# Loads of the head in portions between SyncE's waits, and two visits of the retention part moved

## The chip, the cores and the metric

The kernel runs on one core of one Trainium2 chip. The metric is device time in microseconds (us) of one execution. The kernel before takes 954.64 us, the median of 3 runs (953.72 to 954.76).

## The reference, cut to what matters

```python
# attention part: B, H, S, D = 8, 8, 576, 64; no softmax
scores = scale * np.matmul(q, k.transpose(0, 1, 3, 2))
Dmat = np.where(rel >= 0, gamma[:, None, None] ** rel[None, :, :], 0.0)
attn_out = np.matmul(scores * Dmat[None], v)
x = attn_out.transpose(0, 2, 1, 3).reshape(B * S, H * D)     # 4608 tokens x 512
# dense part: w_in 512 x 2048, w_out 2048 x 512
h = x @ w_in
P = a[0] + a[1] * h + a[2] * h**2 + a[3] * h**3
Q = 1.0 + abs(b[0]) * abs(h) + abs(b[1]) * h**2
out = (P / (Q + 1e-06)) @ w_out
```

Decay by a power of gamma makes the attention part a retention: it can be worked off in pieces that hand on a state.

## The kernel before, in words

**Units.** The 4608 tokens are 36 units of 128 tokens. Unit k is loaded by two DMAs of 512 KB on SyncE's queue (`load_unit`, L115 and L117): `qk` holds q and k, transposed, and `kv` holds k and v. GpSimd scales q (`scale_q`), ScalarE scales v in 8 instructions, one a head (`scale_v`). TensorE then makes the unit's *scores* (from `qk`, in two halves of 64 tokens) and its *state* terms (from `kv`); in the function names both together are the visit of k. VectorE masks the scores and adds up the states (`decay`, `middle`, `add`), GpSimd fades the state by gamma (`fade`). TensorE makes the *outputs* of the unit from the masked scores, v, q and the state (`put`). ScalarE rounds them to a tile `xhi` (`keep_hi`), VectorE keeps the rest in `xlo` (`keep_lo`). Four units are one block of 512 tokens, the x of the dense part.

**Dense part.** It goes in 144 steps, one for each block and each of 16 slices of d_ff: 8 slices of block 0 (steps 0 to 7), all 16 of block 1 (8 to 23), the other 8 of block 0 (24 to 31), then the other blocks. A step makes h (`gemm1`, 12 matmuls of 128x512, from `xhi` and `xlo` with the weight's two parts), runs the rational function on ScalarE and VectorE (`ffn_p`, `ffn_p2`, `ffn_va`, `ffn_v`, `ffn_r`, `ffn_q`, `ffn_q3`), rounds the result to `g` (`ffn_hi`, `ffn_lo`), and three to four steps later multiplies it by w_out (`gemm2`, 12 matmuls). PSUM has two buffers `h`, which the visits of the dense part use as well (as `y`).

**Weights.** They come as float64 bits, 32 tiles `bits` of 512 KB (`load_weights`, L150), and each is converted once (`split_weight`): ScalarE takes the absolute value into `c`, VectorE makes a TENSOR_SCALAR and two SCALAR_TENSOR_TENSOR on it, ScalarE copies it to `w`, GpSimd subtracts to get the second part. `start` and `split0` to `split3` in the order lists are these moves; STARTS_BEFORE and STARTS say how many conversions begin in each step.

**Head.** Before the dense part, `before(n)` for n = 0 to 4 makes the scores of unit n and the outputs of unit n-1, by the list BEFORE, and for the last n by LAST_BEFORE: `visit_a` is the scores of unit n, `visit_b` the outputs of unit n-1. Short series of matmuls that nobody reads (`warm`) stand between them.

**Visits.** VISITS says in which step of the dense part the outputs of one unit and the scores of another are made. Steps 8 to 21 have none; there two halves of a PSUM tile of the retention part (tag `at`) hold the `u` of the steps (`free_at`). The list FIRST sets the order within a step up to step 23, DENSE from step 24.

**Queues.** TensorE, ScalarE, VectorE and GpSimd run in the order in which the code names their work. SyncE's DMAs are placed by the scheduler. DMAs on SyncE's queue have eight slots in turn: each waits until the DMA eight before it has landed. In `emit` the matmuls of a unit's outputs run on two row halves of the array at once; where one half writes a PSUM bank that the other writes too, it waits for the other through an empty instruction on SyncE (`nc.sync.nop()` and `follow`, L289). Such a *join* stands in SyncE's queue among the DMAs: it passes only when the DMAs placed ahead of it have been issued.

**Lines.** Compute instructions are all recorded by one helper (L72 in the profile of before), so groups go by tiles. Of loads, L115 and L117 are a unit's, L150 a weight's, L554 is the small `ab`.

Of the kernel before, what the change touches and what calls it, by code (L numbers as in the profile page):

```python
# [30 lines left out]
NP = 4  # L31

BEFORE = "split1 start scale_q scale_v visit_a decay visit_b add fade keep_hi keep_lo split2 split3 split0".split()
LAST_BEFORE = "visit_a visit_b keep_hi keep_lo start split1 decay add fade scale_q scale_v split2 split3 split0".split()
FIRST = (
    "split1 gemm1 visit ffn_p split2 ffn_p2 ffn_hi decay keep_hi ffn_lo gemm2 ffn_r scale_q split3 decay1 add fade keep_lo"
    " start scale_v split0 ffn_q ffn_q3 ffn_va ffn_v"
# [11 lines left out]
).split()  # L49
END = "ffn_r ffn_hi gemm2 ffn_lo ffn_q ffn_q3".split()  # L50

STARTS_BEFORE = [0, 1, 1, 2, 2]
STARTS = [1, 1, 2, 1, 2] + [1] * 19

VISITS = {0: (4, 5), 2: (5, 6), 4: (6, 7), 6: (7, None), 22: (None, 8)}
FIRST_DENSE = 22
VISITS |= {24 + 2 * i: (8 + i, 9 + i) for i in range(3)}
VISITS |= {30 + 4 * i: (11 + i, 12 + i if i < 24 else None) for i in range(25)}
WARM = [8, 3, 2]
# [16 lines left out]
def retention_ffn(ctx: ExitStack, tc: tile.TileContext, qkv, w_in, w_out, ab, masks, gq, gv, out):  # L76
# [10 lines left out]
    nc = tc.nc  # L87
# [21 lines left out]
    def load_unit(n):  # L109


        late = 2 <= n < 6
        pools = [(wts, f"w{w}_{10 + n}") if late else (raw, "qk" if w == 0 else "kv") for w in range(2)]
        qk = pools[0][0].tile([P, 2, NPAIR, P], F32, tag=pools[0][1], name=f"qk{n}")
        nc.sync.dma_start(qk, qkv[n, :, 0:1024].rearrange("p (a g i) -> p a g i", a=2, g=NPAIR))  # L115
        kv = pools[1][0].tile([P, 2, H, D], F32, tag=pools[1][1], name=f"kv{n}")
        nc.sync.dma_start(kv, qkv[n, :, 1024:2048].rearrange("p (a h d) -> p a h d", a=2, h=H))  # L117
        raws[n] = qk, kv
# [4 lines left out]
    ab_sb = const.tile([P, 6], F32, name="ab_sb")  # L123
# [6 lines left out]
    def warm(n, by=None):  # L130
        by = gq_sb[:, 0] if by is None else by
        for _ in range(n):
            pe.matmul(unread[:, 0:P], by, by, start=True, stop=True)
# [13 lines left out]
    def load_weight(k):  # L147

        bits[k] = wts.tile([P, DM], I64, tag=f"w{k[0]}_{k[1]}", name=f"bits{k[0]}_{k[1]}")
        nc.sync.dma_start(bits[k], (w_in, w_out)[k[0]][k[1]])  # L150
# [39 lines left out]
    def scale_q(n):  # L190

        q = raws[n][0][:, 0]
        pool.tensor_tensor(q, q, gq_sb, ALU.mult)
# [102 lines left out]
    def visit(a, k):  # L296


        places(a, k)
        if a is None:  # L300
            emit(of_scores(k, 0) + of_state(k, 0), of_scores(k, 1) + of_state(k, 1))
        elif k is None:
            put(a)
        else:
            one = of_inside(a, 0, 0) + of_before(a, 0) + of_scores(k, 0) + of_state(k, 0)
            two = of_inside(a, 1, 1) + of_before(a, 1) + of_scores(k, 1) + of_state(k, 1) + of_inside(a, 1, 0)
            one += [[]] * (len(two) - len(one) - 2) + of_inside(a, 0, 1)
            emit(one, two)
        if a is not None:
            done_with(a)  # L310

    def put(a):
        emit(*(of_inside(a, j, j) + of_before(a, j) + of_inside(a, j, 1 - j) for j in range(2)))

    def done_with(a):

        del raws[a]
        state.pop(a, None)
        if 6 <= a + 2 < NU:
            load_unit(a + 2)  # L320
# [185 lines left out]
    def load_weights(n):  # L506
        for k in [k for _, k in zip(range(n), loads)]:
            load_weight(k)
# [12 lines left out]
    def run(names, todo):  # L521
        todo |= {f"split{j}": (split_step, j) for j in range(4)}
        for name in names:
            if name in todo:
                todo[name][0](*todo[name][1:])

    def before(n):
        def start_scores():
            visit(None, n)
            if n + 1 < len(WARM):  # L530
                warm(WARM[n + 1])

        def start_outputs():
            put(n - 1)
            done_with(n - 1)
            if n < NP:
                warm(WARM_OUT)

        todo = {"visit_a": (start_scores,), "start": (split_start, STARTS_BEFORE[n])}
        todo |= {f.__name__: (f, n) for f in (decay, add, fade)}  # L540
        todo |= {f.__name__: (f, n + 1) for f in (scale_q, scale_v)}
        if n >= 1:
            todo |= {f.__name__: (f, n - 1) for f in (keep_hi, keep_lo)}
            todo["visit_b"] = (start_outputs,)
        run(BEFORE if n < NP else LAST_BEFORE, todo)

    nc.sync.dma_start(gq_sb, gq)
    load_unit(0)
    nc.sync.dma_start(gv_sb, gv)
    nc.sync.dma_start(mask_sb, masks)  # L550
    for n in range(1, 6):
        load_unit(n)
        load_weights(1 if n < 3 else 2)
    nc.sync.dma_start(ab_sb, ab)  # L554
    scale_q(0)
    scale_v(0)
    for n in range(NP + 1):
# [11 lines left out]
    for i in range(len(steps) + lag(len(steps))):  # L569
        this, prev, prev2 = (steps[j][:2] if 0 <= j < len(steps) else None for j in (i, i - 1, i - 2))  # L570
        todo = {"gemm2": (products, i), "start": (split_start, STARTS[i] if i < first else 0)}

        if i in VISITS:
            a, k = VISITS[i]
            todo["visit"] = visit, a, k
            if a is not None:
                todo |= {f.__name__: (f, a) for f in (keep_hi, keep_lo)}
            if k is not None:
                todo |= {f.__name__: (f, k) for f in (decay, decay1, add, fade)}
        if i + 1 in VISITS and VISITS[i + 1][1] is not None:  # L580
            todo |= {f.__name__: (f, VISITS[i + 1][1]) for f in (scale_q, scale_v)}
        if this:
# [53 lines left out]
```

## Time and profile before

| | |
|---|---|
| median of 3 runs | 954.64 us (953.72 to 954.76) |
| the profiled execution's own time | 955.94 us |
| its span, first to last instruction | 954.2 us |
| mean granted TensorE clock | 0.975 |
| DMA issues: units, weights, outputs | 72 and 32 of 512 KB, 16 and 4 of 512 and 256 KB |
| moved in the first three fortieths of the span | 334, 406, 334 GB/s |

A row of the timeline gives start, duration, engine, line, operation, output<-input, count, and in brackets how long the engine had been idle before it and what ended that. A row of the waits gives engine, tile, what it waited for, us in total, times and the longest. A row of the stages gives for each engine its busy time and number of instructions, then the granted clock, the share of the DMA engines and GB/s. PEld is TensorE's weight load, SPq SyncE's queue.

### The profile page before, as it was taken

The page shows a single profiled execution, that of the slowest core. Times are in us where ns is not written, and L with a number is a line of the kernel's source. Part 1 is how long each engine was busy: PE and PEld are TensorE (multiplying, and loading weights), DVE is VectorE, ACT ScalarE, POOL GpSimd, SP SyncE. Part 2 cuts the span into 40 slices and gives each one's busy share as a digit, 9 for nine tenths or more (in the row PEclk, how much of TensorE's full clock was granted, in tenths as well). Part 3 has the DMA queues.
Part 4 walks back from the last instruction along what each step waited for, and adds up shares of the span by engine and source line. Part 5 has one row for each costly group of instructions (what it writes and reads, how often), then busy time and mean ns, then how long its engine had stood idle before and what let it go on. Part 6 is the DMA issues. An engine that isn't in the chain of part 4 may idle for free.

```text
span 954.2 us, 19371 instructions
## 1 busy us (share of the span) xinstructions
PE 903.1 (95%) x7852; PEld 739.4 (77%) x7852; DVE 824.8 (86%) x1252; ACT 710.4 (74%) x1274; POOL 152.8 (16%) x128
## 2 busy tenths in 40 slices
PE   5769879979999999999999999999999999999998
PEld 4647658867888888888888888888888888888886
DVE  1699998988999898888888888888898889888895
ACT  3567688867777777877787778877877787867775
POOL 2354344434100000000000000000000000000000
PEclk9779999989999999999999999999999999999999
DMA  9981100001312111211121112111211121001001
GB/s 334 406 334 45 45 1 1 1 1 45 133 45 90 45 45 46 89 45 45 46 89 45 46 46 89 45 46 45 89 45 45 45 89 46 1 1 45 1 1 44
DMA packets 20568, 65.50 MB, mean 69 GB/s; under 512 B 2432, under 2 KB 2432, under 8 KB 20480
## 3 DMA queue, kind: packets, MB, share of 16 engines
q1 hardware_dynamic: 20480, 64.28, 18.9%
q8 instruction: 61, 1.00, 0.4%
q14 instruction: 27, 0.22, 0.1%
HBM read 54.83 MB, written 9.44 MB: 67 GB/s over the span
## 4 chain that ended last, share of the span: by engine, by line
PE 71%; DVE 4%; ACT 3%; issue 1%; DVEq 0%; ACTq 0%; SPq 0%
PE acc L72 34%; PE h L72 32%; PE ps L72 3%; PE y L72 2%; DVE p L72 1%; DVE v L72 1%; ACT kv L72 1%; ACT u L72 1%; DVE g L72 0%; DVE c L72 0%; DVE qk L72 0%; ACT v L72 0%; DVE xlo L72 0%; ACT p L72 0%; ACT g L72 0%
## 5 line engine op out<-in xcount | busy, mean ns | idle before, releaser
L72 PE MATMUL acc<-w,g 128*128 128x512 f32 x1632 | 401.9, 395 | 4.9 <-ACT o L72 3.6
L72 PE MATMUL h<-xhi,w 128*128 128x512 f32 x1152 | 384.0, 395 | 18.2 <-DVE p L72 17.5
L72 PEld LDWEIGHTS acc<-w,g 128*128 128x128 f32 x1632 | 307.1, 190 | 72.3 <-ACT o L72 4.1
L72 PEld LDWEIGHTS h<-xhi,w 128*128 128x128 f32 x1152 | 218.4, 190 | 71.9 <-DVE p L72 25.6
L72 PE MATMUL h<-xlo,w 128*128 128x512 f32 x576 | 226.1, 393 | 0.2 <-DVE xlo L72 0.2
L72 ACT ACTIVATE p<-h,ab_sb 128x512 f32<-128x512 f32 x144 | 111.4, 773 | 83.2 <-PE h L72 77.0
L72 ACT ACTIVATE u<-h 128x512 f32<-128x512 f32 x131 | 78.2, 597 | 89.0 <-DVE v L72 88.5
L72 DVE SCALAR_TENSOR_TENSOR p<-p,ab_sb,u 128x512 f32<-128x512 f32 x131 | 120.0, 916 | 25.8 <-ACT u L72 20.5
L72 PEld LDWEIGHTS h<-xlo,w 128*128 128x128 f32 x576 | 109.3, 190 | 22.5 <-DVE xlo L72 0.5
L72 DVE TENSOR_TENSOR v<-v,u 128x512 f32<-128x512 f32 x131 | 94.4, 721 | 28.3 <-ACT v L72 28.3
L72 DVE TENSOR_TENSOR p<-p,h 128x512 f32<-128x512 f32 x144 | 98.9, 686 | 19.6 <-ACT u L72 19.4
L72 DVE SCALAR_TENSOR_TENSOR p<-p,ab_sb,h 128x512 f32<-128x512 f32 x144 | 107.5, 747 | 4.7
L72 ACT ACTIVATE v<-u,absb 128x512 f32<-128x512 f32 x131 | 105.3, 804 | 0.5
L72 DVE SCALAR_TENSOR_TENSOR p<-v,p 128x512 f32<-128x512 f32 x144 | 99.5, 691 | 4.5
L72 POOL TENSOR_TENSOR S<-S,gv_sb 128x256 f32<-128x256 f32 x32 | 20.1, 629 | 492.8 <-DVE S L72 492.6
L72 ACT ACTIVATE u<-u,lnb 128x512 f32<-128x512 f32 x131 | 94.9, 724 | 4.3
L72 ACT ACTIVATE u<-v,lnb 128x512 f32<-128x512 f32 x131 | 93.3, 712 | 2.0 <-DVE v L72 1.9
L72 ACT ACTIVATE g<-p 128x512 fp32r<-128x512 f32 x136 | 85.7, 630 | 10.5 <-DVE p L72 4.2
L72 DVE SCALAR_TENSOR_TENSOR v<-v,u 128x512 f32<-128x512 f32 x131 | 91.6, 699 | 0.0
L72 DVE TENSOR_TENSOR g<-p,g 128x512 fp32r<-128x512 f32 x112 | 78.8, 703 | 1.4 <-ACT g L72 1.4
L72 ACT ACTIVATE kv<-kv,gv_sb 128x64 f32<-128x64 f32 x288 | 72.4, 335 | 8.3 <-DMA gv_sb<-in_gv 6.6
L72 POOL TENSOR_TENSOR qk<-qk,gq_sb 128x512 f32<-128x512 f32 x36 | 58.4, 1623 | 54.1 <-DMA qk<-in_qkv 54.1
(72 smaller groups left out, 730.0 us busy)
## 6 DMA issues: line engine op xcount, KB each, us to landing
qk<-in_qkv SPq DMA_DIRECT2D x36, 512.0 KB, 4.0
kv<-in_qkv SPq DMA_DIRECT2D x36, 512.0 KB, 5.8
bits<-in_w_in SPq DMA_DIRECT2D x16, 512.0 KB, 10.2
bits<-in_w_out SPq DMA_DIRECT2D x16, 512.0 KB, 10.1
out<-o SPq DMA_DIRECT2D x16, 512.0 KB, 3.7
out<-o SPq DMA_DIRECT2D x4, 256.0 KB, 2.6
gq_sb<-in_gq SPq DMA_DIRECT2D x1, 256.0 KB, 2.8
mask_sb<-in_masks SPq DMA_DIRECT2D x1, 32.0 KB, 6.2
```

Source lines behind the costliest of these rows:

```text
L72: return lambda *a, **k: self.tc.keep_in_program_order(method(*a, **k))
```

## The change

The head's loads, all issued ahead of the first unit's work before, are split in five portions (LOADS): one ahead, and one after each unit's outputs, so that in the code each portion stands behind a join; the small `ab` goes with the third. One conversion moves from n = 3 to n = 4 (STARTS_BEFORE). For n = 4 the outputs of unit 3 come ahead of the scores of unit 4 (LAST_BEFORE), and the order of two rounding steps follows. The scores of unit 8 move from step 22 to step 23 (VISITS); those of unit 9 stay in step 24.

```diff
-LAST_BEFORE = "visit_a visit_b keep_hi keep_lo start split1 decay add fade scale_q scale_v split2 split3 split0".split()
+LAST_BEFORE = "visit_b keep_hi visit_a keep_lo start split1 decay add fade scale_q scale_v split2 split3 split0".split()
...
-STARTS_BEFORE = [0, 1, 1, 2, 2]
+STARTS_BEFORE = [0, 1, 1, 1, 3]
+LOADS = [("u1", 1, "u2", 1, "u3", 1), ("u4", 1), (3,), ("u5", 1), (2,)]
...
-VISITS = {0: (4, 5), 2: (5, 6), 4: (6, 7), 6: (7, None), 22: (None, 8)}
+VISITS = {0: (4, 5), 2: (5, 6), 4: (6, 7), 6: (7, None), 23: (None, 8)}
...
         def start_outputs():
             put(n - 1)
             done_with(n - 1)
+            load_more(n)
+            if n == 2:
+                nc.sync.dma_start(ab_sb, ab)
             if n < NP:
                 warm(WARM_OUT)
...
+    def load_more(n):
+        for what in LOADS[n]:
+            load_weights(what) if isinstance(what, int) else load_unit(int(what[1:]))
...
-    for n in range(1, 6):
-        load_unit(n)
-        load_weights(1 if n < 3 else 2)
-    nc.sync.dma_start(ab_sb, ab)
+    load_more(0)
```

Below are three places of the program's order. Names carry buffer numbers: `qk4`, `kv4` are the loads of unit 4, `bits0_3` is slice 3 of w_in, `bits1_0` slice 0 of w_out. First SyncE's queue in the head; a join is not a row of its own, it shows as `PE_49` among the waits of the DMA behind it, and `DMAHW` is the slot. Before:

```order
L150 DMA bits0_2_137<-in_w_in 128x512 [waits DMAHW5_49]
L150 DMA bits0_3_139<-in_w_in 128x512 [waits DMAHW6_49]
L115 DMA qk4_141<-in_qkv 128x1024 [waits DMAHW7_49]
L117 DMA kv4_143<-in_qkv 128x1024 [waits DMAHW0_49]
L150 DMA bits1_0_145<-in_w_out 128x512 [waits DMAHW1_49]
L150 DMA bits0_4_147<-in_w_in 128x512 [waits DMAHW2_49]
L115 DMA qk5_149<-in_qkv 128x1024 [waits DMAHW3_49]
L117 DMA kv5_151<-in_qkv 128x1024 [waits DMAHW4_49]
L150 DMA bits1_1_153<-in_w_out 128x512 [waits DMAHW5_49]
L150 DMA bits0_5_155<-in_w_in 128x512 [waits DMAHW6_49]
L554 DMA ab_sb_98<-in_ab 128x6 [waits DMAHW7_49]
L150 DMA bits1_2_689<-in_w_out 128x512 [waits PE_49,DMAHW0_49]
```

The first join stands here between `ab` and `bits1_2`.

After, the same queue, from the same load on:

```order
L151 DMA bits0_2_137<-in_w_in 128x512 [waits DMAHW5_49]
L116 DMA qk4_271<-in_qkv 128x1024 [waits PE_49,DMAHW6_49]
L118 DMA kv4_273<-in_qkv 128x1024 [waits DMAHW7_49]
L151 DMA bits0_3_275<-in_w_in 128x512 [waits DMAHW0_49]
L151 DMA bits1_0_368<-in_w_out 128x512 [waits DMAHW1_49]
L151 DMA bits0_4_370<-in_w_in 128x512 [waits DMAHW2_49]
L151 DMA bits1_1_372<-in_w_out 128x512 [waits PE_49,DMAHW3_49]
L539 DMA ab_sb_98<-in_ab 128x6 [waits DMAHW4_49]
L116 DMA qk5_468<-in_qkv 128x1024 [waits DMAHW5_49]
L118 DMA kv5_470<-in_qkv 128x1024 [waits DMAHW6_49]
L151 DMA bits0_5_472<-in_w_in 128x512 [waits DMAHW7_49]
L151 DMA bits1_2_520<-in_w_out 128x512 [waits PE_49,DMAHW0_49]
```

The first join now stands right behind `bits0_2`, the second five loads further on and the third five more; before, ten loads stood between `bits0_2` and the first.

Second, ScalarE in the head, from the scaling of unit 3 to the rounding of unit 3. Before:

```order
L72 ACTIVATE kv3_135<-kv3_135,gv_sb_96 128x64 x8
L72 ACTIVATE xhi0_296<-psNone_1_228 128x4x128
L72 ACTIVATE w0_0_390<-c0_0_217 128x512
L72 ACTIVATE c0_2_395<-bits0_2_137 128x512
L72 ACTIVATE c0_3_397<-bits0_3_139 128x512
L72 ACTIVATE kv4_143<-kv4_143,gv_sb_96 128x64 x8
L72 ACTIVATE xhi0_296<-psNone_2_313 128x4x128
L72 ACTIVATE w0_1_485<-c0_1_302 128x512
L72 ACTIVATE xhi0_296<-psNone_3_408 128x4x128
```

After:

```order
L73 ACTIVATE kv3_135<-kv3_135,gv_sb_96 128x64 x8
L73 ACTIVATE xhi0_283<-psNone_1_209 128x4x128
L73 ACTIVATE w0_0_384<-c0_0_198 128x512
L73 ACTIVATE c0_2_389<-bits0_2_137 128x512
L73 ACTIVATE kv4_273<-kv4_273,gv_sb_96 128x64 x8
L73 ACTIVATE xhi0_283<-psNone_2_300 128x4x128
L73 ACTIVATE w0_1_483<-c0_1_289 128x512
L73 ACTIVATE xhi0_283<-psNone_3_400 128x4x128
L73 ACTIVATE c0_3_551<-bits0_3_275 128x512
```

One conversion's first instruction (`c0_3`) moves from between the second and third rounding to behind the fourth.

Third, TensorE at steps 22 and 23 (`h1_14` and `h1_15` are the h of these steps, `psNone_8` the visit of unit 8, `acc1` the product with w_out). Before:

```order
L72 MATMUL h1_14_1988<-xhi1_670,w0_14_1806 128x512
L72 MATMUL psNone_8_2001<-qk8_1018 64x64 x16
L72 MATMUL psNone_8_2001<-kv8_1020 64x64 x8
L72 MATMUL acc1_0_0_1514<-w1_10_1757,g1_10_1901 128x512 x6
L72 MATMUL acc1_0_1_1515<-w1_10_1757,g1_10_1901 128x512 x6
L72 MATMUL acc1_0_0_1514<-w1_11_1855,g1_11_1950 128x512 x6
L72 MATMUL acc1_0_1_1515<-w1_11_1855,g1_11_1950 128x512 x6
L72 MATMUL h1_15_2078<-xhi1_670,w0_15_1904 128x512
```

After, from the end of the h of step 23:

```order
L73 MATMUL h1_15_2050<-xlo1_672,w0_15_1904 128x512
L73 MATMUL h1_15_2050<-xhi1_671,w0_15_1904 128x512
L73 MATMUL psNone_8_2063<-qk8_1022 64x64 x16
L73 MATMUL psNone_8_2063<-kv8_1024 64x64 x8
L73 MATMUL acc1_0_0_1514<-w1_12_1967,g1_12_2000 128x512 x6
L73 MATMUL acc1_0_1_1515<-w1_12_1967,g1_12_2000 128x512 x6
L73 MATMUL h0_8_2136<-xhi0_283,w0_8_1351 128x512
```

The visit now stands 24 products with w_out and one h later, and one product of 12 and one h ahead of the next visit.

## The prediction

> **What bounds the kernel now.** I read the page's head first, then the stages, then TensorE's waits, then the timeline where the change lies.
>
> ```profile
> span 954.2 us, 19371 instructions
> 20.00:25.00 5.00, 0.42 (x16) 0.42 (x16) 0.00 (x0) 0.00 (x0) 0.34 (x1) 0.50 1.02 409
> 35.00:40.00 5.00, 3.88 (x104) 3.43 (x108) 2.79 (x7) 3.31 (x11) 2.61 (x4) 0.69 1.02 406
> 200.00:220.00 20.00, 17.30 (x118) 14.20 (x121) 15.14 (x22) 12.24 (x27) 7.21 (x6) 0.83 0.01 1
> 320.00:340.00 20.00, 20.00 (x208) 16.62 (x207) 17.66 (x26) 14.74 (x28) 2.32 (x2) 1.00 0.04 15
> ```
>
> TensorE is busy 20.00 of 20.00 us in the late stages, so what an early stage saves comes out at the end. In 20 to 25 us all engines nearly stand still while the DMA engines are full (1.02, 409 GB/s). TensorE's waits up to 260 us, three rows of them:
>
> ```profile
> PE h L72 <- DVE p L72: 17.5, 7, 5.0
> PE psNone L72 <- SPq L289: 9.5, 3, 7.8
> PE psNone L72 <- issue: 5.1, 1, 5.1
> ```
>
> The second row is the joins on SyncE, one of them 7.8 us. The third is one wait at a visit. The first, VectorE freeing an h, is none that the change takes away. SyncE's queue and TensorE at the long join:
>
> ```profile
> 9.82 1.60 SPq L150 DMA_DIRECT2D bits<-in_w_in  x2
> 15.77 0.97 PE L72 MATMUL psNone<-qk,kv 64*64 64x64 f32 x32
> 20.29 0.33 SPq L117 DMA_DIRECT2D kv<-in_qkv  x1
> 24.14 0.33 SPq L554 DMA_DIRECT2D ab_sb<-in_ab  x1
> 24.58 0.70 PE L72 MATMUL psNone<-qk,kv 64*64 64x64 f32 x16 [7.84 <-SPq L289]
> ```
>
> The first row is the issue of `bits0_2` and `bits0_3`. From 20.29 to 24.14 SyncE issues a load each (24.14-20.29)/3 = 1.28 us, since each waits for the landing of the eighth before it. TensorE is through at 15.77+0.97 = 16.74, its join stands behind `ab`, and it goes on at 24.58.
>
> **The change part by part.** *The first join.* Ahead of it now stand only the loads up to `bits0_2`, issued by 9.82+1.60 = 11.4, so SyncE is at the join before TensorE (16.74). The other two waits of the row sum to 9.5-7.8 = 1.7, so a join with a short queue costs under 0.9, and I give it 0.3. TensorE ends the outputs of unit 0 at about 17.5. What is late next is not TensorE but the load of unit 3: `kv5` is issued at 20.29 because `kv3` landed then, and nothing ahead of `kv3` changes. The rest of the head is a chain of ScalarE and VectorE:
>
> ```profile
> 26.40 2.01 ACT L72 ACTIVATE kv<-kv,gv_sb 128x64 f32<-128x64 f32 x8
> 31.49 0.60 ACT L72 ACTIVATE xhi<-psNone 128x512 fp32r<-128x512 f32 x1 [3.08 <-PE psNone L72]
> 37.11 0.57 ACT L72 ACTIVATE xhi<-psNone 128x512 fp32r<-128x512 f32 x1
> 39.09 0.63 ACT L72 ACTIVATE w<-c 128x512 fp32r<-128x512 f32 x1 [1.42 <-DVE c L72]
> 41.26 0.60 ACT L72 ACTIVATE xhi<-psNone 128x512 fp32r<-128x512 f32 x1 [1.53 <-PE psNone L72]
> 41.89 0.69 DVE L72 TENSOR_TENSOR xlo<-psNone,xhi 128x512 fp32r<-128x512 f32 x1 [2.22 <-ACT xhi L72]
> ```
>
> The scaling of unit 3 now runs at 20.29 to 22.3 (2.01 us), and the second rounding follows at 22.3, 9.2 earlier than 31.49; its own input is ready before (outputs of unit 1, about 21). From the second to the third rounding it was 37.11-31.49 = 5.62; of this one conversion's first instruction leaves (it moves behind the fourth rounding; row 13.02 below, 0.66), so the third comes at 22.3+5.0 = 27.3. The copy of a weight follows 39.09-37.11 = 1.98 later, at 29.3, and the fourth rounding directly behind it at 29.9, since the outputs of unit 3 no longer wait for the scores of unit 4: that takes out the 1.53 of the row 41.26. TensorE keeps up: those outputs need the masked scores of unit 3, done near 27, and a join behind `bits0_6`, whose slot is that of `bits1_0`, landed near 26.7. So the last `xlo` starts at 29.9+0.63 = 30.5 instead of 41.89, **11.4 earlier**.
>
> From `xlo` on VectorE has no pause until TensorE gets an h back:
>
> ```profile
> 13.02 0.66 ACT L72 ACTIVATE c<-bits 128x512 f32<-128x512 f32 x1
> 26.59 0.42 DVE L72 TENSOR_SCALAR c<-c 128x512 int32<-128x512 int32 x1
> 46.25 2.90 DVE L72 TENSOR_SCALAR c<-c 128x512 int32<-128x512 int32 x2
> 47.41 2.86 POOL L72 TENSOR_TENSOR w<-c,w 128x512 fp32r<-128x512 f32 x2
> 53.15 0.73 DVE L72 SCALAR_TENSOR_TENSOR p<-p,ab_sb,h 128x512 f32<-128x512 f32 x1
> 53.94 0.80 PE L72 MATMUL h<-xhi,w 128*128 128x512 f32 x1 [5.04 <-DVE p L72]
> ```
>
> In this stretch, 41.89 to 53.88, stand the same VectorE instructions as before and one more: the conversion that begins later has its TENSOR_SCALAR here, 0.42. The head's gain at TensorE's row 53.94 is 11.4-0.4 = **11.0**. Two TENSOR_SCALAR beside GpSimd took 2.90, not 2x0.42, so one costs up to (2.90-0.84)/2 = 1.03 more when GpSimd is on the same ground; but before, two `w` of GpSimd fell into the stretch, and now one, the other coming a step later. I put that at nothing, with -2 to +1 as bounds of the head's gain.
>
> [...]
>
> Loads: the DMA queue must not run dry. The first portion lands until 20.29+1.28 = 21.6 (`bits0_2`), and the second is issued from 17 on, behind the join; the later ones come with eight in flight. The stream goes on at 1.28 a load, and unit 4's `kv` lands second behind that, at 24.1 (ScalarE reaches it at 27.3-2.0 = 25.3), the last of the three conversions' bits fifth, at 28.0 (reached near 32), unit 5's `kv` eighth, with `ab` near 32.0 (reached at 30.5+3x0.66 = 32.5). That last cover is thin, 0.5; without it ScalarE is late by as much, and VectorE, which has eleven instructions to do there first, is not.
>
> The clock: granted 0.50 behind the 7.84 wait, as in the stage 20 to 25. With it gone the series run at full clock:
>
> ```profile
> 26.79 1.13 PE L72 MATMUL psNone<-qk 64*64 64x64 f32 x32
> 32.22 0.69 PE L72 MATMUL psNone<-qk 64*64 64x64 f32 x32
> 37.21 0.37 PE L72 MATMUL unread<-gq_sb 128*128 128x128 f32 x1 [1.12 <-issue]
> ```
>
> But in 35 to 40 the clock was 0.69 with no wait over 1.12, so a head with short waits can also fall to half: 0.44 for each of some five series, 2.2 at TensorE, most of it in the shade of the ScalarE chain; I charge nothing and allow 1. [...]
>
> *Unit 8's visit.*
>
> ```profile
> 197.19 0.39 PE L72 MATMUL h<-xhi,w 128*128 128x512 f32 x1
> 199.83 2.01 ACT L72 ACTIVATE kv<-kv,gv_sb 128x64 f32<-128x64 f32 x8
> 201.93 0.68 DVE L72 SCALAR_TENSOR_TENSOR v<-v,free_at 128x512 f32<-128x512 f32 x1
> 202.70 1.13 PE L72 MATMUL psNone<-qk 64*64 64x64 f32 x32 [5.12 <-issue]
> 204.60 7.13 PE L72 MATMUL acc<-w,g 128*128 128x512 f32 x24
> 206.80 0.68 DVE L72 TENSOR_TENSOR qk<-psNone,mask_sb 128x512 f32<-128x512 f32 x1
> 207.38 0.80 ACT L72 ACTIVATE v<-u,absb 128x512 f32<-128x512 f32 x1
> 208.07 0.48 DVE L72 TENSOR_SCALAR c<-c 128x512 int32<-128x512 int32 x1
> 214.56 0.78 ACT L72 ACTIVATE p<-h,ab_sb 128x512 f32<-128x512 f32 x1 [6.37 <-PE h L72]
> 215.92 0.69 DVE L72 TENSOR_TENSOR p<-p,h 128x512 f32<-128x512 f32 x1 [4.19 <-ACT u L72]
> 225.62 0.50 PE L72 MATMUL h<-xhi,w 128*128 128x512 f32 x1 [0.60 <-DVE p L72]
> ```
>
> TensorE stood 5.12 us until VectorE had read the last `free_at` (201.93+0.68 = 202.61), since the visit takes that PSUM tile; then ScalarE 6.37 and VectorE 4.19 for the next h. Now TensorE goes from 197.4 into the 24 products (7.13 at most, as in the row) and the h of step 23 (12 matmuls, half of that), and is through by 208.1 at the latest. ScalarE is next: it has unit 8's scaling in step 22 now, 2.01 ahead of its `v`, so `v` runs at 209.4 and `p` of step 23 at 210.2 instead of 214.56, 4.4 earlier. VectorE follows at 211.5 for 215.92. Behind it come the three mask and state instructions of unit 8, 208.07-206.80 = 1.3 long, which move here from step 22: 4.4-1.3 = **3.1** is left. TensorE's h of step 25, which waits for VectorE at 225.62, comes that much earlier, and behind it TensorE is the bound. TensorE gets a new wait at the moved visit, up to about 209.4 for ScalarE's scaling; nothing is behind it that VectorE's chain would not hold as long. Bounds: the whole wait with the half clock behind it, 5.1+1.4, and, if the scaling of unit 8 comes onto the path while nothing else is won, -2.0.
>
> Sum: 11.0+3.1 = 14.1. The profiled execution's span 954.2 becomes 940.1 (its own time, 955.94, has 1.7 around the span, which stay); the median 954.64 lies 1.3 under that own time, and on it I forecast: 954.64-14.1 = 940.5.
>
> **The rivals.** *Unit 8's scaling takes the wait's place.* For it: ScalarE sits between both visits, and they are now one step apart, not two, so that mask, state and scaling of units 8 and 9 follow each other without slack. Against: ScalarE idles 6.37 there now. It gives 954.64-11.0 = 943.6.
>
> *Three TENSOR_SCALAR in a row each meet GpSimd* (scaling of unit 5, then a `w`). Each loses 1.03: 3.1, so 940.5+3.1 = 943.6. Against it, GpSimd's two operations there last less than that together with what before already paid. [...]
>
> *Slower: the queue runs dry.* Each portion is issued only when TensorE has reached a join, and TensorE waits for loads. Were a portion issued after the last load before it has landed, each would cost an unhidden load. In section 6 of the page a unit's `kv` takes this from issue to landing:
>
> ```profile
> kv<-in_qkv SPq DMA_DIRECT2D x36, 512.0 KB, 5.8
> ```
>
> Four portions at 5.8 are 23.2 against 14.1 won: 954.64+9.1 = 963.7. It decides from the point where the second portion is issued later than 21.6; I have it at 17, a margin of 4.5, and each later portion has more in flight.
>
> *The change doesn't do what it says*, because the scheduler, which places SyncE's DMAs, puts the loads ahead of the joins again: 954.6. The order of the queue speaks against it: `PE_49` stands at `qk4`.
>
> **How the numbers follow.** Forecast 0.62; unit 8's scaling 0.17; the lock 0.14; queue dry 0.04; no effect 0.03. The range takes the forecast with its bounds (head 8.5 to 12, visit 0.7 to 5) and the next two rivals: 954.64-17 = 937.6 to 954.64-9.2 = 945.4. A measurement of this kernel can tell about 0.2% (1.9 us) from no change. Faster by more: 0.62+0.17+0.14 = 0.93; within it 0.03; slower 0.04.
>
> **What would show it.** In the profile after, TensorE's wait on SyncE near 16.7 should be under 1 us, the last `xlo` of the head should start near 30.5, TensorE's second h near 43, and the wait at unit 8's visit should be one on ScalarE, under 4 us. It is wrong if the DMA engines pause in the first 40 us, if the gain near 43 is under 8, or if the 11 us seen there are not seen at 190: then something between has a bound of its own.

## The result, and the profile after

The changed kernel takes 940.78 us, the median of 4 runs (940.24 to 941.99); the kernel before took 954.70 us beside it (4 runs, 953.72 to 955.11). The ratio is 0.9857, with a 95% interval of 0.9840 to 0.9874: 13.9 us less, against 14.1 forecast. In the table below the ratios are to the kernel before, run on the same chip. One execution of `starts_back` took 1947 us, with TensorE's `acc` matmul at 0.73 us on average for 0.39; it is left out of the medians and of what follows.

| kernel | median us | ratio to before (95%) |
|---|---|---|
| the changed kernel | 940.78 | 0.9857 (0.9840 to 0.9874) |
| loads_alone | 947.61 | 0.9931 (0.9918 to 0.9943) |
| visit_alone | 949.93 | 0.9949 (0.9937 to 0.9962) |
| visit_back | 945.88 | 0.9910 (0.9897 to 0.9924) |
| swap_back | 941.70 | 0.9868 (0.9854 to 0.9881) |
| starts_back, starts_again | 942.51, 941.73 | 0.9876 (0.9860 to 0.9893), 0.9866 (0.9850 to 0.9883) |
| no_warm | 940.09 | 0.9851 (0.9836 to 0.9865) |
| unit3_first | 941.22 | 0.9861 (0.9845 to 0.9877) |
| scale_early | 941.86 | 0.9868 (0.9854 to 0.9883) |
| thin_loads | 939.03 | one execution |
| nowarm_unit3 | 939.45 | 0.9846 (0.9831 to 0.9861) |
| held_loads | 939.11 | 0.9845 (0.9831 to 0.9858) |

The page's head and the stages of the profile after; the columns are those of the first fence of the prediction.

```profile
span 938.5 us, 19369 instructions
20.00:25.00 5.00, 2.03 (x64) 1.77 (x65) 3.79 (x8) 3.58 (x13) 1.49 (x2) 0.80 1.02 404
30.00:35.00 5.00, 4.88 (x118) 4.37 (x118) 1.79 (x3) 2.42 (x6) 1.27 (x1) 0.67 0.95 331
320.00:340.00 20.00, 20.00 (x208) 16.32 (x207) 17.75 (x28) 14.91 (x26) 2.31 (x2) 1.00 0.17 54
```

In 20 to 25 us, where before nearly nothing ran, VectorE and ScalarE are now busy for 3.79 and 3.58 of 5 us. The DMA engines are as full as before (1.02), and TensorE's clock is 0.80 there and 0.67 from 30 to 35. The late stage is full, as it was. TensorE's waits up to 260 us:

```profile
PE psNone L73 <- POOL qk L73: 5.0, 2, 2.5
PE psNone L73 <- issue: 3.6, 2, 3.0
PE unread L73 <- issue: 1.8, 1, 1.8
```

The joins on SyncE (9.5 us before) and the 5.1 us at unit 8's visit are gone. New are 2.5 us for GpSimd's `qk` at that visit, and three pauses in the head that the profile puts to "issue": TensorE waits there for nothing that the profile shows. The head along its critical engines, from the timeline:

```profile
17.15 0.50 PE L73 MATMUL psNone<-qk 64*64 64x64 f32 x18 [0.60 <-issue]
19.50 2.02 ACT L73 ACTIVATE kv<-kv,gv_sb 128x64 f32<-128x64 f32 x8 [1.53 <-DMA kv<-in_qkv]
21.42 0.57 ACT L73 ACTIVATE xhi<-psNone 128x512 fp32r<-128x512 f32 x1
23.54 1.01 PE L73 MATMUL psNone<-qk 64*64 64x64 f32 x25 [2.97 <-issue]
27.31 0.60 ACT L73 ACTIVATE xhi<-psNone 128x512 fp32r<-128x512 f32 x1 [0.80 <-PE psNone L73]
29.83 0.37 PE L73 MATMUL unread<-gq_sb 128*128 128x128 f32 x1 [1.83 <-issue]
32.58 0.60 ACT L73 ACTIVATE xhi<-psNone 128x512 fp32r<-128x512 f32 x1 [2.63 <-PE psNone L73]
33.21 0.69 DVE L73 TENSOR_TENSOR xlo<-psNone,xhi 128x512 fp32r<-128x512 f32 x1 [3.64 <-ACT xhi L73]
44.54 0.80 PE L73 MATMUL h<-xhi,w 128*128 128x512 f32 x1 [5.18 <-DVE p L73]
```

The third rounding stands at 27.31, as forecast (27.3). The fourth does not: it waits 2.63 for TensorE, which has lost 0.60, 2.97 and 1.83 us in its pauses. So the last `xlo` is at 33.21, not 30.5, 2.7 late. The stretch from there to the second h, which was to get 0.4 longer, got 0.7 shorter (11.33 for 12.05), and so the second h comes at 44.54, 9.4 earlier than 53.94 and not 11.0.

From there the lead can be read off ScalarE's `p<-h`, one a step: 9.4 us in steps 3 to 12, 11.0 in steps 16 to 21, and 15.8 in step 26. The step from 9.4 to 11.0 is this pair, of before and of after, where TensorE waits for ScalarE to read a finished `acc`:

```profile
140.09 5.49 PE L72 MATMUL acc<-w,g 128*128 128x512 f32 x12 [3.64 <-ACT o L72]
```

```profile
130.69 3.04 PE L73 MATMUL acc<-w,g 128*128 128x512 f32 x12 [3.62 <-ACT o L73]
```

Behind the same wait the 12 matmuls ran at half clock in the one profile (0.50 granted from 140 to 145) and at full clock in the other (1.00 from 130 to 135). So 1.6 us of the 15.7 between the two spans are of that kind. They are no part of the change: in 13 profiles of this case (all but that of `starts_back`) this wait is 3.59 to 3.64 long, and the 12 matmuls behind it took 5.4 to 5.5 us in seven, 4.2 to 4.6 in five, and 3.04 in the changed kernel's alone. Variants of before and of after are in both groups. Two of these spans thus differ by up to 1.6 us at this one place.

### The profile page after: what moved, and what is told of

Read it like the earlier page. It is cut to its first block, busy times and chain, and to the rows that moved or that the text cites. A ratio compares the mean times of both kernels' runs of the same rounds, so it can differ in the third digit from the quotient of the medians.

```text
span 938.5 us, 19369 instructions
## 1 busy us (share of the span) xinstructions
PE 899.4 (96%) x7852; PEld 737.2 (79%) x7852; DVE 825.0 (88%) x1252; ACT 710.2 (76%) x1274; POOL 153.0 (16%) x128
## 4 chain that ended last, share of the span: by engine, by line
PE 46%; DVE 28%; ACT 20%; issue 4%; DMA 1%; POOL 0%; SPq 0%; DVEq 0%; ACTq 0%; POOLq 0%
PE h L73 21%; PE acc L73 20%; DVE p L73 14%; DVE v L73 7%; ACT u L73 6%; ACT v L73 4%; ACT g L73 3%; ACT kv L73 3%; DVE c L73 3%; ACT free_at L73 2%; PE psNone L73 2%; PE ps L73 2%; DVE qk L73 1%; DVE g L73 1%; DVE xlo L73 1%
## 5 line engine op out<-in xcount | busy, mean ns | idle before, releaser
L73 DVE TENSOR_TENSOR v<-v,u 128x512 f32<-128x512 f32 x131 | 95.0, 725 | 28.5 <-ACT v L73 28.5
L73 DVE TENSOR_TENSOR p<-p,h 128x512 f32<-128x512 f32 x144 | 98.9, 687 | 14.5 <-ACT u L73 14.2
```

Of the source, the lines that this page charges most:

```text
L73: return lambda *a, **k: self.tc.keep_in_program_order(method(*a, **k))
```

## The experiments

### The parts alone

**loads_alone**: the changed kernel with everything but the portions as before.

```diff
-LAST_BEFORE = "visit_b keep_hi visit_a keep_lo start split1 decay add fade scale_q scale_v split2 split3 split0".split()
+LAST_BEFORE = "visit_a visit_b keep_hi keep_lo start split1 decay add fade scale_q scale_v split2 split3 split0".split()
-STARTS_BEFORE = [0, 1, 1, 1, 3]
+STARTS_BEFORE = [0, 1, 1, 2, 2]
-VISITS = {0: (4, 5), 2: (5, 6), 4: (6, 7), 6: (7, None), 23: (None, 8)}
+VISITS = {0: (4, 5), 2: (5, 6), 4: (6, 7), 6: (7, None), 22: (None, 8)}
```

> The loads in portions alone; the conversions' starts, the order of step 4 and the visit of unit 8 as before. By the prediction's terms the head gives 11.0 - 1.5 (order of step 4) - 0.7 + 0.4 (starts) = 9.2: about 945.5 us, and the last xlo of the head starts near 32.7. Rival, read from the changed kernel's trace: TensorE itself is late in the head (its pauses of 2.97 and 1.83 us, and half clock behind them), so the scores of unit 4 (1.08 + 0.69) come on top of that: 9.4 - 1.8 = 7.6, about 947.1 us, last xlo near 35. The same 'issue' pauses should stand in TensorE's rows of the head.

Measured: 947.61, 7.0 less than before. The fourth rounding:

```profile
33.52 0.60 ACT L73 ACTIVATE xhi<-psNone 128x512 fp32r<-128x512 f32 x1 [3.73 <-PE psNone L73]
```

The time is nearer to the rival's (947.1): TensorE, waited for 3.73 us, is late at the fourth rounding. The last `xlo` starts at 34.15, between the two forecasts (32.7 and 35). The pauses stand at the same tiles with 2.70 and 2.00.

**visit_alone**: the kernel before, with `23: (None, 8)` for `22: (None, 8)`. **visit_back**: the changed kernel with `22: (None, 8)`.

> Unit 8's visit in step 23 alone, all else as before. By the prediction 3.1 us less: about 951.6 us. Rival, from the changed kernel's trace (there TensorE waits 2.49 for GpSimd's qk at the visit, and the 12 products behind it take 5.49 at half clock where 2.88 is the full-clock time): only 1.9 less, about 952.8 us.

> The changed kernel with unit 8's visit in step 22 again. By the prediction 3.1 us more than the changed kernel: about 943.9 us, and TensorE waits about 5 us at the visit again. Rival: 1.9 more, about 942.7 us.

Measured: 949.93, 4.7 less than before, and 945.88, 5.1 more than the changed kernel. Both forecasts were too low. ScalarE's `p<-h` of steps 21, 23 and 24 in the kernel before, and then in `visit_alone`:

```profile
193.83 0.79 ACT L72 ACTIVATE p<-h,ab_sb 128x512 f32<-128x512 f32 x1
...
214.56 0.78 ACT L72 ACTIVATE p<-h,ab_sb 128x512 f32<-128x512 f32 x1 [6.37 <-PE h L72]
222.06 0.76 ACT L72 ACTIVATE p<-h,ab_sb 128x512 f32<-128x512 f32 x1
```

```profile
192.52 0.78 ACT L72 ACTIVATE p<-h,ab_sb 128x512 f32<-128x512 f32 x1
...
208.38 0.76 ACT L72 ACTIVATE p<-h,ab_sb 128x512 f32<-128x512 f32 x1
...
215.95 0.76 ACT L72 ACTIVATE p<-h,ab_sb 128x512 f32<-128x512 f32 x1
```

The lead is 1.3 ahead of the visit (193.83-192.52), 6.2 behind it (214.56-208.38) and still 6.1 in step 24 (222.06-215.95). So the visit gives 4.8, and the mask and state instructions, which step 23 now has in addition, take nothing of it. Why not is seen on VectorE between two `p` of step 23, before and then in `visit_alone`:

```profile
218.24 0.73 DVE L72 SCALAR_TENSOR_TENSOR p<-p,ab_sb,h 128x512 f32<-128x512 f32 x1
219.57 1.42 DVE L72 TENSOR_SCALAR c<-c 128x512 int32<-128x512 int32 x1 [0.60 <-ACT c L72]
220.92 0.74 DVE L72 SCALAR_TENSOR_TENSOR p<-p,ab_sb,u 128x512 f32<-128x512 f32 x1
```

```profile
212.11 0.74 DVE L72 SCALAR_TENSOR_TENSOR p<-p,ab_sb,h 128x512 f32<-128x512 f32 x1
212.77 0.68 DVE L72 TENSOR_TENSOR qk<-psNone,mask_sb 128x512 f32<-128x512 f32 x1
213.37 0.40 DVE L72 TENSOR_TENSOR kv<-S,psNone 128x256 f32<-128x256 f32 x1
213.70 0.41 DVE L72 TENSOR_TENSOR qk<-psNone,mask_sb 128x256 f32<-128x256 f32 x1
214.03 0.83 DVE L72 TENSOR_SCALAR c<-c 128x512 int32<-128x512 int32 x1
214.79 0.74 DVE L72 SCALAR_TENSOR_TENSOR p<-p,ab_sb,u 128x512 f32<-128x512 f32 x1
```

Both take 2.68 us from the first `p` to the second (220.92-218.24, 214.79-212.11). The three instructions fill the 0.60 in which VectorE waited for ScalarE's `c`, and the TENSOR_SCALAR behind them takes 0.83 instead of 1.42; why it is shorter was not followed.

**swap_back**: the changed kernel with LAST_BEFORE of before. **starts_back** and **starts_again** (the same kernel twice): with STARTS_BEFORE of before.

> The changed kernel with the order of step 4 as before (unit 4's scores and mask ahead of unit 3's outputs and rounding). By the prediction 1.5 us more: 942.3 us, last xlo 1.5 later than 33.21. If TensorE paces the head, 1.8 more (its 32 score and 16 state products at half clock stand ahead of the outputs) and the rounding's wait on TensorE grows from 2.63 by as much. Rival: nothing changes, if the pauses of TensorE have another cause that swallows it.

> The changed kernel with the conversions started 0, 1, 1, 2, 2 as before. By the prediction's terms 0.7 - 0.4 = 0.2 us more (one ScalarE instruction of 0.66 ahead of the third rounding, one TENSOR_SCALAR of 0.42 fewer behind the last xlo): 941.0 us. Rival, since TensorE and not ScalarE is waited for at the last rounding (2.63 in the changed kernel): the 0.66 is hidden, and only VectorE's 0.42 to 0.9 is won: 939.9 to 940.4 us. With it the three parts of the head come to 7.0 (loads alone) + 0.9 (order of step 4) + this one, of about 9.0.

> The same kernel as starts_back, for a usable profile: 942.6 us again. Its head is expected 1 to 2 us later than the changed kernel's at TensorE's second h (44.54). If the two conversions ahead of the fourth rounding cost it on ScalarE, the last xlo is late by as much; if they cost VectorE, the stretch from the last xlo to p of the first h is longer than 10.54.

Measured: 941.70 for `swap_back`, 0.9 more than the changed kernel, and 942.51 and 941.73 for the other, 1.7 and 0.9 more. All these intervals overlap that of the changed kernel. In `swap_back` the last rounding waited 3.65 for TensorE (2.63 in the changed kernel). TensorE's third pause, the last rounding, the last `xlo` and the second h of `starts_again`:

```profile
29.27 0.27 PE L73 MATMUL unread<-gq_sb 128*128 128x128 f32 x1 [1.73 <-issue]
31.29 0.60 ACT L73 ACTIVATE xhi<-psNone 128x512 fp32r<-128x512 f32 x1 [1.52 <-PE psNone L73]
31.92 0.69 DVE L73 TENSOR_TENSOR xlo<-psNone,xhi 128x512 fp32r<-128x512 f32 x1 [2.21 <-ACT xhi L73]
43.98 0.79 PE L73 MATMUL h<-xhi,w 128*128 128x512 f32 x1 [5.04 <-DVE p L73]
```

From the last `xlo` to the second h it is 12.06, as in the kernel before (12.05), where the changed kernel has 11.33 (44.54-33.21): with the starts of before VectorE needs 0.7 more, and no loss shows on ScalarE. But the second h was not 1 to 2 us late, as expected; it came 0.6 earlier than in the changed kernel, because TensorE went on 0.6 earlier behind its third pause (29.27 for 29.83) and was 0.7 faster from there to the last rounding (2.02 for 2.75, where the changed kernel ran at half clock, 0.51 granted from 29.8 to 32.6). So this trace does not show the loss in time, and whether the order of step 4 or the starts are worth anything alone is open. The four parts add up to 7.0+0.9+4.7 = 12.6 and 0.9 to 1.7 for the starts, that is 13.5 to 14.3 for 13.9; with two terms that are not clear of the noise this does not show whether the parts help or hinder one another.

### What TensorE's pauses are

In the changed kernel 127 matmul records lie between the pauses at 23.54 and 29.83, and as many between 17.15 and 23.54. With the weight load of each matmul this is 254 instructions.

**no_warm**: 28 records fewer in the head.

```diff
-WARM = [8, 3, 2]
-WARM_OUT = 3
+WARM = [8, 0, 0]
+WARM_OUT = 0
```

> The changed kernel without the products on 'unread' in the head but the first eight: 28 TensorE records fewer. If TensorE's 'issue' pauses are the fetch of its next block of instructions (in the changed kernel they stand 127 matmul records apart), they stay 127 apart and move in the program: from 13 records into unit 2's scores to 29 into them, from 6 records into unit 3's scores to 28, and from the products on 'unread' behind unit 2's outputs to 27 records into unit 3's outputs; their lengths of about 0.6, 3.0 and 1.8 stay. Rival: they come from the waiting data or from the clock, then they stay at the same tiles or go with the products. The time: 940 to 942 us, with a lower granted clock in the head if the products held it up.

Measured: 940.09. The timeline of TensorE at the three pauses, each with the row ahead of it:

```profile
15.13 0.68 PE L73 MATMUL psNone<-qk 64*64 64x64 f32 x29
17.53 0.33 PE L73 MATMUL psNone<-qk 64*64 64x64 f32 x3 [1.71 <-issue]
...
20.51 1.04 PE L73 MATMUL psNone<-qk 64*64 64x64 f32 x28
23.64 0.33 PE L73 MATMUL psNone<-qk 64*64 64x64 f32 x4 [2.09 <-issue]
...
26.74 0.63 PE L73 MATMUL psNone<-qk,S 64*64 64x64 f32 x11
29.93 0.38 PE L73 MATMUL psNone<-qk,S 64*64 64x64 f32 x3 [2.56 <-issue]
```

The pauses come after 29 and 28 records of the scores of units 2 and 3, and in unit 3's outputs after 16 of `qk,kv` and 11 of `qk,S`, which is 27: at all three places as counted beforehand. Only their lengths did not stay (1.71, 2.09, 2.56; 6.4 in all against 5.4). So they go by the number of instructions. What stays nearly the same is when TensorE goes on, at 17.53, 23.64 and 29.93 for 17.15, 23.54 and 29.83: TensorE needs 3.4 to 4.5 us for the 127 matmuls, but the next ones begin 6.1 to 6.4 us after the last 127 began, and the pause is what is left of that. That the pauses are the fetch of a next block of instructions is up to here an estimate from the 127; `held_loads` below has the transfers.

**thin_loads** was to leave the DMA engines idle when the third block comes, by later portions.

```diff
-LOADS = [("u1", 1, "u2", 1, "u3", 1), ("u4", 1), (3,), ("u5", 1), (2,)]
+LOADS = [("u1", 1, "u2", 1, "u3", 1), ("u4",), ("u5",), (), (7,)]
```

> The changed kernel with the head's loads thinned out: behind the first portion only unit 4's two, then unit 5's two, and all seven remaining weight blocks with the last portion. The DMA engines should then have only some five loads in flight near 20.5 and none near 26 to 28. If TensorE's 'issue' pauses are instruction blocks that arrive behind the loads, the third (1.83) falls under 0.5 and the second (2.97) gets shorter; if the fetch takes that long by itself, or the pauses have another cause, both stay as they are. The kernel's time is not the question (the weights come late): 941 to 950 us.

Measured: 939.03, pauses of 2.97 and 1.74. It tells nothing on the question, since the loads did not thin out. The scheduler placed the weights of the last portion further ahead in SyncE's queue, and the stage 25 to 30 was as full as ever:

```profile
25.00:30.00 5.00, 3.17 (x88) 2.58 (x86) 2.53 (x6) 1.77 (x5) 2.08 (x3) 0.82 1.02 403
```

**held_loads** does the same by a dependency that the scheduler has to keep: each load behind unit 5's follows the last matmul of unit 2's outputs.

```diff
-LOADS = [("u1", 1, "u2", 1, "u3", 1), ("u4", 1), (3,), ("u5", 1), (2,)]
+LOADS = [("u1", 1, "u2", 1, "u3", 1), ("u4",), ("u5",), (7,), ()]
...
             put(n - 1)
             done_with(n - 1)
+            if n == 3:
+                gate[:] = last_mm
             load_more(n)
...
-        nc.sync.dma_start(bits[k], (w_in, w_out)[k[0]][k[1]])
+        d = nc.sync.dma_start(bits[k], (w_in, w_out)[k[0]][k[1]])
+        if gate:
+            follow(d, gate[0])
```

> The changed kernel with only units 4 and 5 loaded in the middle of the head; every load behind them waits for the end of unit 2's outputs (about 27), so that the DMA engines stand still from about 26 to 28. If TensorE's 'issue' pauses are instruction blocks that arrive behind the loads, the third (1.83 in the changed kernel, near 28) falls under 0.5, while the second (2.97 near 20.6, with the queue still full) stays above 2. If a block takes that long by itself, or the pauses have another cause, both stay. The time is a by-product: the weights land later, 940 to 946 us.

Measured: 939.11. Stages and timeline of `held_loads`:

```profile
20.00:22.00 2.00, 0.07 (x6) 0.00 (x0) 1.59 (x5) 1.28 (x5) 0.61 (x1) 1.00 1.04 406
24.00:26.00 2.00, 1.91 (x79) 1.70 (x70) 1.44 (x3) 2.00 (x9) 2.00 (x3) 1.00 0.09 29
```

```profile
23.05 0.62 PE L73 MATMUL psNone<-qk 64*64 64x64 f32 x25 [2.98 <-issue]
26.60 0.27 PE L73 MATMUL unread<-gq_sb 128*128 128x128 f32 x1 [0.40 <-issue]
29.38 0.46 PE L73 MATMUL psNone<-qk,kv 64*64 64x64 f32 x16 [1.66 <-SPq L298]
29.91 0.60 ACT L73 ACTIVATE xhi<-psNone 128x512 fp32r<-128x512 f32 x1 [1.56 <-PE psNone L73]
30.54 0.69 DVE L73 TENSOR_TENSOR xlo<-psNone,xhi 128x512 fp32r<-128x512 f32 x1 [2.58 <-ACT xhi L73]
```

With the queue full (1.04) the second pause is 2.98, as in the changed kernel; with the DMA engines at 0.09 the third is 0.40 instead of 1.83. The table of DMA queues has transfers of the kind "instruction": on q8 the changed kernel's page counts 61 with 1.00 MB, beside 15704 instructions of TensorE (7852 matmuls and as many weight loads), 257 to a transfer, near the 254 between two pauses. So these are read here as TensorE's blocks of instructions: TensorE waits for its next one, and it comes late because of the loads. A block's transfer as a row (queue, kind, packets, MB, share) was found at 20.75 to 21.0 and 27.25 to 27.5 in the changed kernel, and at 24.0 to 24.25 in `held_loads`:

```profile
q8 instruction: 1, 0.02, 27.0%
q8 instruction: 1, 0.02, 26.7%
```

```profile
q8 instruction: 1, 0.02, 25.0%
```

TensorE had begun the block before it at 17.15 and 23.54 in the changed kernel, at 23.05 in `held_loads`: the transfer begins 3.6 to 4.0 us later with a full queue, 1.0 to 1.2 without. From there to TensorE's next matmul (23.54, 29.83 and 26.60) it is another 2.3 to 2.8 in all three cases, so this part does not come from the loads: from the begin of one block to that of the next it takes 6.4 and 6.3 us behind the loads, and still 3.6 without them. The 1.66 on SyncE is the price of holding the loads back: a join again stands behind the issue of loads. Even so the last `xlo` starts at 30.54; in this execution unit 3's scaling also began 0.7 earlier (18.78 for 19.50). By time `held_loads` can't be told from the changed kernel, as the intervals overlap.

### Which engine is waited for

**unit3_first**: unit 3's loads ahead of the second weight's. **nowarm_unit3**: this and `no_warm` together.

```diff
-LOADS = [("u1", 1, "u2", 1, "u3", 1), ("u4", 1), (3,), ("u5", 1), (2,)]
+LOADS = [("u1", 1, "u2", "u3", 1, 1), ("u4", 1), (3,), ("u5", 1), (2,)]
```

> The changed kernel with unit 3's two loads ahead of the second weight's: kv3 lands 1.28 us earlier. If the landing of kv3 and ScalarE's chain behind it set the head, as the prediction has it, 1.3 us less: 939.5 us. If TensorE with its pauses sets the last rounding, nothing (940.8 us): the second and third rounding come 1.3 earlier and the wait on TensorE before the fourth grows from 2.63 to 3.9.

> The changed kernel without the head's products on 'unread' and with unit 3's loads ahead of the second weight's, the two edits that alone gave 940.1 and 941.2. If TensorE's blocks of instructions set the last rounding, this stays at 940 to 941 us; if the products on 'unread' had been what held TensorE behind kv3's landing, up to 1.3 less, 938.8 us.

Measured: 941.22, not to be told from the changed kernel, and 939.45. ScalarE in `unit3_first`:

```profile
20.26 0.67 ACT L73 ACTIVATE c<-bits 128x512 f32<-128x512 f32 x1 [2.88 <-DMA bits<-in_w_in]
20.84 2.00 ACT L73 ACTIVATE kv<-kv,gv_sb 128x64 f32<-128x64 f32 x8
...
32.31 0.60 ACT L73 ACTIVATE xhi<-psNone 128x512 fp32r<-128x512 f32 x1 [1.94 <-PE psNone L73]
```

The expectation had overlooked that a conversion stands ahead of unit 3's scaling on ScalarE: its bits now land later, and the scaling begins at 20.84 for 19.50. ScalarE was made 1.3 later, not earlier, and still the last rounding did not move (32.31 for 32.58): TensorE sets it. `nowarm_unit3` lies 1.3 below the changed kernel with overlapping intervals; whether it is faster is open.

**scale_early**: unit 8's scalings in step 21.

```diff
-        if i + 1 in VISITS and VISITS[i + 1][1] is not None:
-            todo |= {f.__name__: (f, VISITS[i + 1][1]) for f in (scale_q, scale_v)}
+        ahead = 23 if i == 21 else i + 1
+        if i != 22 and ahead in VISITS and VISITS[ahead][1] is not None:
+            todo |= {f.__name__: (f, VISITS[ahead][1]) for f in (scale_q, scale_v)}
```

> The changed kernel with unit 8's scalings in step 21 instead of 22. TensorE's wait of 2.49 for GpSimd's qk at the visit goes, and the half clock behind it (5.49 for 12 products instead of 2.88). If ScalarE's order in step 22 (2.00 of scaling ahead of p of step 23) sets the pace, 2.0 us less: 938.8 us. Rival: VectorE's chain sets it, and TensorE's wait is off the path: 940.8 us.

Measured: 941.86. TensorE's wait of 2.49 at the visit is gone and its 12 products there take 3.02, yet nothing is won, and TensorE waits at the next visit instead (waits of 180 to 235 us):

```profile
PE ps L73 <- DVE qk L73: 3.1, 1, 3.1
```

So the new wait at the moved visit was off the path, as the prediction said, and VectorE's chain is what sets it.

## Why the prediction was right, and where it was not

*The total* is right, 13.9 for 14.1, but by luck: its two terms are off by about 2 us each, in opposite directions. The range takes the visit up to 5, where its working allows 5.1+1.4 = 6.5; nothing hangs on that here, though `visit_back` measured 5.1.

*The join* went as said: no wait on SyncE is left in the head. The chain on ScalarE up to the third rounding has the right order and, by luck, the right time (27.3 forecast, 27.31 measured): it began 0.8 earlier, with unit 3's landing, and waited 0.80 for TensorE.

*"TensorE keeps up"* is the step that failed. The term of 11.0 measured 9.4 in the profile, and 9.0 by the runs (13.9 less the visit's 4.9, the mean of 4.7 and 5.1). What took its place is the fetch of TensorE's instructions behind the loads. Before, TensorE passed the first two of the three block ends without a pause, since the joins had held it back: it came to them in unit 2's and unit 3's scores (the rows 26.79 and 32.22 in the prediction), and the blocks' transfers (one on q8 each) lie before that, at 14.5 to 15 and 28 to 28.5 us. The third was the row 37.21 with 1.12 "issue", which the prediction quoted and took for a matter of the clock. The half clock that the prediction allowed for came too, and is the smaller part: behind the third pause it cost the changed kernel's profile 0.7 of the 2.7 (2.75 for 2.02, by `starts_again`), and `no_warm`, which had 0.50 in 25 to 35, took no longer.

The term put at nothing behind the last `xlo`, one `w` of GpSimd less beside VectorE, was worth something: the stretch is 11.33, where 12.05 and the one instruction more make 12.5, and with the starts of before it is 12.06. That gave back 1.1 of the 2.7; that it is this `w` was not tried by itself.

*The order of step 4* was said to be worth 1.5 and measured 0.9; *the conversions' starts* were to give 0.2 and measured 0.9 and 1.7. Neither is clear of no effect, nor of its forecast.

*Unit 8's visit*: 3.1 forecast, 4.7 and 5.1 measured. The 4.4 for ScalarE's `p` was near (4.9 in `visit_alone`). The subtraction of 1.3 for mask and state was the failed term: they found 0.60 of idle time, and the TENSOR_SCALAR behind them took 0.59 less. The wait at the moved visit was 2.49, within the 4 us allowed, though GpSimd and not ScalarE ended it.

*The signs.* The second h was 1.5 later than the 43 named, and the last `xlo` 2.7 later than 30.5. The 11 us that were to be seen at 190 were seen there, 11.0, but by luck: 9.4 were the head's, and 1.6 came with the clock on the way.

*The rivals.* The scaling of unit 8 did not take the wait's place (`scale_early`). The three TENSOR_SCALAR in a row did take longer than alone (0.42, row 26.59 of the prediction), as the two of before did beside GpSimd (VectorE in the head of the changed kernel):

```profile
35.95 3.67 DVE L73 TENSOR_SCALAR c<-c 128x512 int32<-128x512 int32 x3
```

Three took 3.67 where two took 2.90, with GpSimd at work beside them (`S`, `qk` and `w`, 35.60 to 39.33). No run shows the lock to which the prediction gives 0.14, and that it is GpSimd that slows them was not tried by itself; the runs show only these times. But from the last `xlo` to the second h it is 11.33 and was 12.05 (53.94-41.89), so the stretch as a whole got no longer by it. The queue did not run dry: from 10 to 40 us, no stage of 5 us had the DMA engines busy under 0.95.

## What to carry to other kernels

TensorE's short instructions had a supply line of their own in this head: 127 matmuls at a time, with 6.1 to 6.4 us from one begin to the next while the DMA queues were full (the changed kernel and `no_warm`), and 3.6 us in `held_loads` with the DMA engines at 0.09. So count an engine's short instructions in the stretch where the DMA queues are full, and look whether its pauses stand equally many of them apart. Compare when it goes on, not how long it pauses: in `no_warm`, work taken away ahead of such ends only made the pauses longer, 6.4 us in all for 5.4. A wait that is taken away may have been hiding such a fetch, as the joins of before did (9.5 us), and an "issue" row in the trace of before (1.12 here) is the hint. An instruction that moves onto a chain need not lengthen it: look for an idle gap behind the place where it lands (0.60 on VectorE here) before its duration is subtracted.

## What the runs showed of the hardware

In these runs TensorE's clock did not follow from the length of the wait alone. It ran at half behind waits of 3.64 (the `o` of before, 0.50 granted) and 2.97 (23.54 in the changed kernel, 25 matmuls in 1.01, 0.50 granted from 23.5 to 24.6), and at full behind 3.62 (the `o` of the changed kernel, 1.00 granted) and 2.98 (23.05 in `held_loads`, the same 25 in 0.62, 1.00 granted from 22 to 24). What sets it was not shown. Such a flip makes up to 1.6 us here, as much as the smaller parts of the change.
